# First tokens' softmax on ScalarE, weight shift on ScalarE, another load order, and last sums that end tile by tile

## The chip, the core and the metric

The kernel runs on one core of a Trainium2 chip. TensorE (PE) multiplies matrices, VectorE (DVE) and ScalarE (ACT) work on tiles, GpSimd (POOL) does a little of that too, and SyncE (SP) issues the transfers (DMA). The metric is the device time of one execution in microseconds; less is better. Three timed runs of the kernel before gave a median of 584.38 us (581.32 to 584.8).

## The reference

Attention over 4 batches, 8 heads, 576 tokens of width 64: a causal softmax, mixed by a gate with a memory read; its output, as 2304 tokens of width 512, goes through two weight layers with a squared ReLU between them. Both weights are float64.

```python
scores = where(causal, -1e9, q @ k.T / 8)
scores = scores - scores.max(-1)
a = exp(scores); a /= a.sum(-1) + 1e-9
phi = lambda x: where(x > 0, x, exp(x) - 1) + 1
mem_out = (phi(q) @ M_prev) / ((phi(q) * z_prev).sum(-1) + 1e-6)
x = g * mem_out + (1 - g) * (a @ v)        # g = sigmoid(beta), per head
r = maximum(x @ w_in, 0); out = (r * r) @ w_out
```

## The kernel before

**Staging.** All loads and stores are issued from SP, in one queue. The first 64 tokens of each batch (the only ones with a 64 x 64 score block) are handled apart in `first_tokens`, in two groups of two batches (g = 0, 1); they are the first block of 256 tokens for the two weight layers, so that TensorE has a block to work on while attention goes on. The other 512 tokens of each batch go through `attention`, in eight blocks of 256 for the layers (`moe`); the last two blocks are done together, 512 tokens wide, in `moe_pair`.

**Weights.** TensorE multiplies in a rounded float32 form, so each weight is split into a high and a low part, and a product is three matmuls (high x high, high x low, low x high). A piece n is 128 x 512 float64, loaded raw, as pairs of 32-bit words. `split_weight` makes a float32 of it: VectorE shifts the low word right by 29 (L163), ScalarE rescales the high word (L164), VectorE joins the two (L165), ScalarE rounds to the high part (L168), VectorE subtracts for the low part (L169). There are 32 pieces: pieces 0 to 3 are w_in and 4 to 7 w_out for the first quarter of the hidden width, and so on. Twelve fit into the first stage (9 `raw` tiles, two `hw`, one `xw` in two halves).

**First tokens.** For each group: `scores` (L265), `phi` (exp at L272, minimum at L273, then products and the gate's scale up to L280), `softmax` (scale and mask L285, maximum L288, subtraction L289, exp L290, sum L291, reciprocal and scale L292 to L295), `outputs` (transposes L304, copies L306, products L315, high part `xh` L319, low part `xl` L320). The two groups fill the two halves of `xh` and `xl`. The first layer matmuls of the first block (`up`, L721 to L723) need both halves: L721 and L723 read `xh`, L722 reads `xl`.

**What sets the order.** A planner places every instruction of all engines at build time, in one fixed order per engine; `first_tokens` has high priority in it, and `merge` interleaves attention, weight pieces and the first block. The loads of the first tokens come in the order that `SEQ` spells: a (q, k), b (q rows and z), c (v and M) of a group, g the gates, r a raw weight piece, l the first attention batch.

**The end.** `moe_pair` adds up four token tiles of 128 x 512 over 16 steps f. Tiles 0 and 1 have PSUM tiles of their own (`oacc`); tiles 2 and 3 are halves of one tile (`oacs`), and a reader of it waits for both. ScalarE copies the sums out (L692) and SP stores them (L694). GpSimd makes the low part `gl` there (L679).

## Time and profile before

| | |
|---|---|
| median of three runs | 584.38 us |
| the profiled execution | 583.52 us, its span 581.7 us |
| granted TensorE clock, mean | 0.997 of full speed |
| PE busy | 544.9 us (94%) |
| DVE, ACT busy | 406.3 us (70%), 349.3 us (60%) |

The span runs from the first to the last instruction; the rest of an execution's time lies around it. A matmul's duration reaches past the start of the next one, so that PE reads as busy when matmuls follow one another without a hole. A duration on the other engines overlaps a little with the next instruction too: what one costs a full queue is the distance from its start to the start of the one behind it. A share over the whole span says little here, since the first 46 us, the middle and the last 5 us have different limits.

### The profile page before, as it was taken

What the parts mean: (1) busy time and instruction counts of PE and PEld (TensorE: products, weight loads), DVE (VectorE), ACT (ScalarE), POOL (GpSimd) and SP (SyncE); (2) the same over time, 40 slices, a digit from 0 to 9 for tenths busy, and PEclk for the clock granted to TensorE, in tenths of its full rate; (3) what the DMA queues carried; (4) which work ended last, traced back from release to release, by engine and by line L of the source; (5) the groups of instructions that cost most, each with busy time, mean ns of one, the idle gap of its engine ahead of it and who ended that gap; (6) DMA issues with size and microseconds to landing.
All of it is one profiled execution on the core that took longest, in us unless ns stands there. A gap on an engine that the chain in (4) does not pass through costs nothing.

```text
span 581.7 us, 11097 instructions
## 1 busy us (share of the span) xinstructions
PE 544.9 (94%) x4019; PEld 469.7 (81%) x4019; DVE 406.3 (70%) x1338; ACT 349.3 (60%) x794; POOL 39.4 (7%) x36
## 2 busy tenths in 40 slices
...
GB/s 283 372 176 368 94 254 194 155 143 158 96 153 135 117 134 189 148 200 155 128 136 95 148 99 155 111 178 139 55 90 114 110 16 1 36 1 0 1 0 73
DMA packets 125462, 75.72 MB, mean 130 GB/s; under 512 B 97248, under 2 KB 110560, under 8 KB 125408
## 3 DMA queue, kind: packets, MB, share of 16 engines
...
q14 instruction: 23, 0.19, 0.1%
...
## 4 chain that ended last, share of the span: by engine, by line
PE 62%; DVE 22%; DMA 9%; ACT 4%; issue 2%; SPq 1%; ACTq 0%; DVEq 0%
PE oacc L713 6%; PE oacc L711 6%; PE oacc L712 6%; PE up L723 6%; PE up L722 6%; PE up L721 6%; PE sp L467 4%; DVE e L486 3%; PE up L672 2%; PE up L671 2%; PE up L670 2%; DVE a L546 2%; DMA aT<-a 2%; DVE w L169 2%; PE pm L435 2%
## 5 line engine op out<-in xcount | busy, mean ns | idle before, releaser
L721 PE MATMUL up<-xh,w 128*128 128x256 f32 x448 | 129.0, 288 | 0.9 <-ACT xh L319 0.7
L723 PE MATMUL up<-xh,w 128*128 128x256 f32 x448 | 129.3, 289 | 0.0
L722 PE MATMUL up<-xl,w 128*128 128x256 f32 x448 | 128.3, 286 | 0.3 <-DVE xl L320 0.3
L506 ACT ACTIVATE e<-e,mx 128x320 f32<-128x320 f32 (+3 forms) x128 | 77.7, 610 | 54.9 <-DVE memx L586 35.4
L721 PEld LDWEIGHTS up<-xh,w 128*128 128x128 f32 x448 | 86.3, 193 | 5.0 <-ACT xh L319 1.0
L711 PE MATMUL oacc<-w,gh 128*128 128x512 f32 x224 | 90.2, 403 | 0.0
L712 PE MATMUL oacc<-w,gh 128*128 128x512 f32 x224 | 88.9, 397 | 0.0
L722 PEld LDWEIGHTS up<-xl,w 128*128 128x128 f32 x448 | 86.2, 192 | 3.0 <-issue 0.6
L723 PEld LDWEIGHTS up<-xh,w 128*128 128x128 f32 x448 | 86.2, 192 | 1.3 <-issue 0.7
L713 PE MATMUL oacc<-w,gl 128*128 128x512 f32 x224 | 85.4, 398 | 0.8 <-DVE gl L733 0.8
L546 DVE SCALAR_TENSOR_TENSOR a<-e,a 128x128 f16<-128x128 f32 x116 | 66.0, 577 | 24.1 <-ACT a L544 23.6
L678 DVE CAST gh<-r 128x512 fp32r<-128x512 f32 x16 | 6.8, 428 | 78.6 <-ACT r L677 78.6
L544 ACT ACTIVATE a<-e 128x128 f16<-128x128 f32 x116 | 55.1, 525 | 9.5 <-DMA aT<-a 9.1
L727 ACT ACTIVATE r<-up 128x512 f32<-128x512 f32 x56 | 32.9, 588 | 42.6 <-PE up L723 25.2
L713 PEld LDWEIGHTS oacc<-w,gl 128*128 128x128 f32 x224 | 40.9, 188 | 9.3 <-DVE gl L733 1.9
L711 PEld LDWEIGHTS oacc<-w,gh 128*128 128x128 f32 x224 | 42.2, 188 | 7.5 <-ACT hw L164 0.8
L712 PEld LDWEIGHTS oacc<-w,gh 128*128 128x128 f32 x224 | 42.3, 189 | 6.6
L486 DVE CUSTOM_DVE_ANT_0 e<-sp,mask 128x320 f32<-128x320 f32 (+3 forms) x128 | 47.2, 415 | 0.0
L676 ACT ACTIVATE r<-up 128x512 f32<-128x512 f32 x16 | 9.6, 599 | 62.1 <-PE up L672 62.1
L679 POOL TENSOR_TENSOR gl<-r,gh 128x512 fp32r<-128x512 f32 x16 | 20.7, 1292 | 379.9 <-DVE gh L678 379.9
L733 DVE TENSOR_TENSOR gl<-r,gh 128x512 fp32r<-128x512 f32 x56 | 39.1, 699 | 2.9 <-ACT gh L730 1.7
L576 PE MATMUL acc<-vs,aT 128*128 128x128 f16 x302 | 36.5, 220 | 0.0
(153 smaller groups left out, 1131.1 us busy)
## 6 DMA issues: line engine op xcount, KB each, us to landing
...
```

Source lines behind the costliest of these rows:

```text
L486: nc.vector.tensor_tensor_reduce(out=e[:, h, ka:kb], in0=sps[:, h, cs], in1=mask[:, 448 - q0 + ka : 448 - q0 + kb], scale=-0.125, scalar=3 ...
L506: ex = nc.scalar.activation(e[:n, h, :ke], e[:n, h, :ke], AF.Exp, bias=bs, scale=-1.0, accum_out=sm[:n, h : h + 1])
L544: nc.scalar.mul(av[:, :, o0 : o0 + w], x, SC)
L546: nc.vector.scalar_tensor_tensor(out=av[:, :, o0 + w : o0 + 2 * w], in0=x, scalar=SC, in1=av[:, :, o0 : o0 + w], op0=ALU.mult, op1=ALU.sub ...
L576: nc.tensor.matmul(o2, aT[:, h * nb + c, :n], vs[:, h, c], start=False, stop=c == i)
L711: nc.tensor.matmul(acc[t], gh[:, u, ts], w_out_op(f, 0), start=f == 0, stop=False)
L712: nc.tensor.matmul(acc[t], gh[:, u, ts], w_out_op(f, 1), start=False, stop=False)
L713: nc.tensor.matmul(acc[t], gl[:, u, ts], w_out_op(f, 0), start=False, stop=f == NF - 1)
L721: nc.tensor.matmul(up[:, u, :], w_in_op(f, k, 0), xh[:, k, :], start=k == 0, stop=False)
L722: nc.tensor.matmul(up[:, u, :], w_in_op(f, k, 0), xl[:, k, :], start=False, stop=False)
L723: nc.tensor.matmul(up[:, u, :], w_in_op(f, k, 1), xh[:, k, :], start=False, stop=k == NK - 1)
L733: (nc.vector if n in GLV else nc.gpsimd).tensor_tensor(out=gl, in0=r, in1=gh.bitcast(F32), op=ALU.subtract)
```

## The change

Five edits, and what the planner makes of them.

- `split_weight`: for pieces 0 to 7 the shift of the low word is done by ScalarE (an Identity activation that reads the word's upper 16 bits and scales them down), for the others by VectorE as before. `half` is its constant bias.
- `phi`: the exp and VectorE's minimum become two ScalarE passes (ReLU of -q, then exp of its negative).
- `softmax`: scores are negated, VectorE takes a minimum instead of a maximum; the subtraction, exp and sum are sixteen ScalarE passes of 64 columns (8 for each group), each with the row's minimum as its bias and a sum as second output. VectorE's subtraction and sum are gone.
- `SEQ`: raw weight pieces are loaded between the tensors of the first tokens.
- `moe_pair`: each of the four token tiles has a PSUM tile of its own; in the last three steps the sums end one tile after another, and each tile is copied out and stored as it ends; `gl` is made by VectorE.

```diff
--- before.py
+++ after.py
@@ -11,6 +11,7 @@
 F16 = mybir.dt.float16
 BF16 = mybir.dt.bfloat16
 U32 = mybir.dt.uint32
+U16 = mybir.dt.uint16
 AF = mybir.ActivationFunctionType
 ALU = mybir.AluOpType
 AX = mybir.AxisListType
@@ -53,7 +54,7 @@
 KB = 1
 XB = 2
 PJ = 6
-SEQ = 'a0 b0 g a1 b1 c0 c1 r l r r r r'
+SEQ = 'a0 b0 g a1 r b1 r c0 l r r c1'
 W0 = 9
 EARLY = 'dp'
 LATE = 'dd'
@@ -104,6 +105,8 @@
     nc.scalar.copy(identr, idt)
     identb = cp.tile([P, P], BF16, name="identb")
     nc.vector.tensor_copy(identb, idt)
+    half = cp.tile([P, 1], F32, name="half")
+    nc.vector.memset(half, 2.0**-14 - 0.5)
     mask = cp.tile([P, MW], BF16, name="mask")
     nc.gpsimd.memset(mask, 0.0)
     nc.gpsimd.affine_select(
@@ -160,7 +163,11 @@
             u0, u1 = rw[:, :, 0], rw[:, :, 1]
             f1 = u1.bitcast(F32)
             hi, lo = wp[n][:, 0, c0:c1], wp[n][:, 1, c0:c1]
-            nc.vector.tensor_scalar(out=u0, in0=u0, scalar1=29, scalar2=None, op0=ALU.logical_shift_right)
+            if n < 8:
+                top = rw.bitcast(U16).rearrange("p n (t h) -> p n t h", h=2)[:, :, 0, 1]
+                nc.scalar.activation(u0, top, AF.Identity, scale=2.0**-13, bias=half[:, :1])
+            else:
+                nc.vector.tensor_scalar(out=u0, in0=u0, scalar1=29, scalar2=None, op0=ALU.logical_shift_right)
             nc.scalar.activation(f1, f1, AF.Prelu, scale=2.0**-111, alpha=-(2.0**32))
             nc.vector.scalar_tensor_tensor(
                 out=u1, in0=u1, scalar=3, in1=u0, op0=ALU.logical_shift_left, op1=ALU.bitwise_or
@@ -269,8 +276,8 @@
             wt0[g] = tp.tile([P, GN, P], F32, tag="w", name="w", bufs=2)
             f = wt0[g][:, :, D:]
             t2 = tp.tile([P, GN], F32, tag="t2", name="t2", bufs=2)
-            nc.scalar.activation(f, qn, AF.Exp)
-            me[g].tensor_scalar(out=f, in0=f, scalar1=1.0, scalar2=None, op0=ALU.min)
+            nc.scalar.activation(f, qn, AF.Relu, scale=-1.0)
+            nc.scalar.activation(f, f, AF.Exp, scale=-1.0)
             nc.vector.scalar_tensor_tensor(out=f, in0=qn, scalar=0.0, in1=f, op0=ALU.max, op1=ALU.add)
             ze[g].tensor_tensor(out=zb, in0=zb, in1=f, op=ALU.mult)
             nc.vector.reduce_sum(out=t2, in_=zb, axis=AX.X)
@@ -283,13 +290,15 @@
             e = wt0[g][:, :, :D]
             t1 = tp.tile([P, GN], F32, tag="t1", name="t1", bufs=2)
             nc.vector.scalar_tensor_tensor(
-                out=e, in0=sp[g], scalar=0.125, in1=mask0[:, None, :].to_broadcast(bc), op0=ALU.mult, op1=ALU.add
+                out=e, in0=sp[g], scalar=-0.125, in1=mask0[:, None, :].to_broadcast(bc), op0=ALU.mult, op1=ALU.subtract
             )
-            nc.vector.reduce_max(out=t1, in_=e, axis=AX.X)
-            xe[g].tensor_tensor(out=e, in0=e, in1=t1[:, :, None].to_broadcast(bc), op=ALU.subtract)
-            nc.scalar.activation(e, e, AF.Exp)
-            nc.vector.reduce_sum(out=t1, in_=e, axis=AX.X)
-            nc.vector.tensor_scalar(out=t1, in0=t1, scalar1=1e-9, scalar2=None, op0=ALU.add)
+            nc.vector.tensor_reduce(out=t1, in_=e, axis=AX.X, op=ALU.min)
+            ts = tp.tile([P, GN], F32, tag="ts", name="ts", bufs=2)
+            for i in range(GN):
+                nc.scalar.activation(
+                    e[:, i], e[:, i], AF.Exp, bias=t1[:, i : i + 1], scale=-1.0, accum_out=ts[:, i : i + 1]
+                )
+            nc.vector.tensor_scalar(out=t1, in0=ts, scalar1=1e-9, scalar2=None, op0=ALU.add)
             nc.vector.reciprocal(t1, t1)
             nc.vector.tensor_tensor(out=t1, in0=t1, in1=g1b, op=ALU.mult)
             ye[g].tensor_tensor(out=e, in0=e, in1=t1[:, :, None].to_broadcast(bc), op=ALU.mult)
@@ -652,17 +661,24 @@
     def moe_pair():
         xs = xq.pop()
         xh, xl = ([x[k // 2][:, k % 2].rearrange("p n c -> p (n c)") for k in range(NK)] for x in xs)
-        acc = [ps.tile([P, DM], F32, tag="acc", name="oacc", bufs=2) for _ in range(2)]
-        more = ps.tile([P, 2, DM], F32, tag="s", name="oacs")
-        acc += [more[:, 0], more[:, 1]]
+        acc = [ps.tile([P, DM], F32, tag=t, name="oacc", bufs=2) for t in ("acc", "acc", "av", "av")]
         pend = []
 
-        def down(f, gh, gl):
-            for t in range(4):
+        def down(f, gh, gl, tokens=range(4)):
+            mms = []
+            for t in tokens:
                 ts = slice(t * P, (t + 1) * P)
-                nc.tensor.matmul(acc[t], gh[:, ts], w_out_op(f, 0), start=f == 0, stop=False)
-                nc.tensor.matmul(acc[t], gh[:, ts], w_out_op(f, 1), start=False, stop=False)
-                nc.tensor.matmul(acc[t], gl[:, ts], w_out_op(f, 0), start=False, stop=f == NF - 1)
+                for g, part, s0, s1 in ((gh, 0, f == 0, False), (gh, 1, False, False), (gl, 0, False, f == NF - 1)):
+                    mms.append(nc.tensor.matmul(acc[t], g[:, ts], w_out_op(f, part), start=s0, stop=s1))
+            return mms
+
+        def evict(t):
+            b, blk = blocks[NBLK - 2 + t // 2]
+            r0 = b * S + QT[1 + 2 * blk + t % 2][0]
+            pool, tag, bufs = (mo, "x", XB) if t < 2 else (at, ("qh", "ql")[t - 2], 1)
+            o = pool.tile([P, DM], F32, tag=tag, name="o", bufs=bufs)
+            nc.scalar.activation(o, acc[t], AF.Copy, scale=WSC)
+            nc.sync.dma_start(out[r0 : r0 + P, :], o)
 
         for f in range(NF):
             up = ps.tile([P, 2 * BLK], F32, tag="up", name="up", bufs=2)
@@ -671,27 +687,32 @@
                 nc.tensor.matmul(up, w_in_op(f, k, 0), xl[k], start=False, stop=False)
                 nc.tensor.matmul(up, w_in_op(f, k, 1), xh[k], start=False, stop=k == NK - 1)
             r = mo.tile([P, 2 * BLK], F32, tag="r", name="r", bufs=RB)
-            gh = mo.tile([P, 2 * BLK], F32R, tag="gh", name="gh", bufs=GHB)
-            gl = mo.tile([P, 2 * BLK], F32R, tag="gl", name="gl", bufs=GLB)
+            if f < NF - 1:
+                gh = mo.tile([P, 2 * BLK], F32R, tag="gh", name="gh", bufs=GHB)
+                gl = mo.tile([P, 2 * BLK], F32R, tag="gl", name="gl", bufs=GLB)
+            else:
+                gh, gl = (at.tile([P, 2 * BLK], F32R, tag=t, name="gz") for t in ("kh", "kl"))
             nc.scalar.activation(r, up, AF.Relu, scale=WSC)
             nc.scalar.activation(r, r, AF.Square)
             nc.vector.tensor_copy(gh, r)
-            nc.gpsimd.tensor_tensor(out=gl, in0=r, in1=gh.bitcast(F32), op=ALU.subtract)
+            nc.vector.tensor_tensor(out=gl, in0=r, in1=gh.bitcast(F32), op=ALU.subtract)
             pend.append((f, gh, gl))
             yield
-            if len(pend) > 1:
+            if f == NF - 2:
+                down(*pend[0], tokens=(2, 3))
+            elif 0 < f < NF - 2:
                 down(*pend.pop(0))
-                yield
-        for x in pend:
-            down(*x)
-        for m in range(2):
-            b, blk = blocks[NBLK - 2 + m]
-            for t in range(2):
-                pool, tag, n = (mo, "x", XB) if m == 0 else (at, ("qh", "ql")[t], 1)
-                o = pool.tile([P, DM], F32, tag=tag, name="o", bufs=n)
-                nc.scalar.activation(o, acc[2 * m + t], AF.Copy, scale=WSC)
-                r0 = b * S + QT[1 + 2 * blk + t][0]
-                nc.sync.dma_start(out[r0 : r0 + P, :], o)
+            yield
+        three, two, one = pend
+        ends = None
+        for x, tokens in ((three, (0, 1)), (two, (0, 1)), (one, (0, 1)), (two, (2,)), (one, (2,)), (two, (3,)), (one, (3,))):
+            mms = down(*x, tokens=tokens)
+            if ends is not None:
+                tc.add_manual_dep(mms[0].ins, ends.ins.name, AFTER, reason="one token tile ends behind another")
+            ends = mms[-1]
+            if x is one:
+                for t in tokens:
+                    evict(t)
         yield
 
     def moe(n):
```

ScalarE, from the first group's exp (before) or the second group's (after) on; `raw` and the numbered `w` tiles are weight pieces, `w` without a number holds the first tokens' phi and softmax, `ts` their sums, `pe` and `e` belong to attention. Before:

```order
L272 ACTIVATE w<-tr_119 128x8x64
L164 ACTIVATE raw_141<-raw_141 128x512
L380 ACTIVATE pe<-qm 128x256
L290 ACTIVATE w<-w 128x8x64 x2
L164 ACTIVATE raw_149<-raw_149 128x512
L168 CAST w_98<-raw_141 128x512
L164 ACTIVATE raw_151<-raw_151 128x512
L164 ACTIVATE raw_153<-raw_153 128x512
L506 ACTIVATE e,sm<-e,mx 128x320
L164 ACTIVATE raw_155<-raw_155 128x512
L506 ACTIVATE e,sm<-e,mx 128x320
L168 CAST w_99<-raw_149 128x512
```

Now:

```order
L279 ACTIVATE w<-tr_121 128x8x64
L280 ACTIVATE w<-w 128x8x64
L175 CAST w_100<-raw_138 128x512
L168 ACTIVATE raw_143<-raw_143,half 128x512
L171 ACTIVATE raw_143<-raw_143 128x512
L298 ACTIVATE w,ts<-w,t_212 128x64 x8
L298 ACTIVATE w,ts<-w,t_260 128x64
L389 ACTIVATE pe<-qm 128x256
L298 ACTIVATE w,ts<-w,t_260 128x64 x4
L175 CAST w_101<-raw_143 128x512
L298 ACTIVATE w,ts<-w,t_260 128x64
L168 ACTIVATE raw_152<-raw_152,half 128x512
L171 ACTIVATE raw_152<-raw_152 128x512
L298 ACTIVATE w,ts<-w,t_260 128x64 x2
```

Between the first two pieces' casts there stood two exps; now there stand two of the new shifts and most of the sixteen pieces, interleaved with the weights.

VectorE, the last rows ahead of the second half of `xl`, which the first full group of `up` matmuls needs. Before:

```order
L444 TENSOR_TENSOR memx<-pm,nm 128x256
L165 SCALAR_TENSOR_TENSOR hw<-hw 128x512
L390 SCALAR_TENSOR_TENSOR pe<-qm,pe 128x256
L486 ISA e,mx<-sp,mask 128x192
L486 ISA mx 128x1
L163 TENSOR_SCALAR hw<-hw 128x512
L486 ISA e,mx<-sp,mask 128x192
L486 ISA mx 128x1
L320 TENSOR_TENSOR xl<-xp,xh 128x4x128
```

Now:

```order
L176 TENSOR_TENSOR w_108<-raw_437,w_108 128x512
L451 RECIPROCAL nm<-nm 128x4
L176 TENSOR_TENSOR w_111<-xw,w_111 128x256 x2
L495 ISA e,mx<-sp,mask 128x192
L495 ISA mx 128x1
L495 ISA e,mx<-sp,mask 128x192
L495 ISA mx 128x1
L176 TENSOR_TENSOR w_109<-hw,w_109 128x512
L399 SCALAR_TENSOR_TENSOR pe<-qm,pe 128x256
L453 TENSOR_TENSOR memx<-pm,nm 128x256
L329 TENSOR_TENSOR xl<-xp,xh 128x4x128
```

Ahead of `xl` stood attention's rows and two rows of one `hw` piece; now the low parts (`L176`) of three weight pieces stand there, and each of them waits for ScalarE's cast of that piece.

TensorE, the last down projections; `gh` and `gl` are the high and low part of a step's squared ReLU, `gz` those of the last step. Before, the last step's rows:

```order
L663 MATMUL oacc<-w_1140,gh 128x512
L664 MATMUL oacc<-w_1140,gh 128x512
L663 MATMUL oacc<-w_1140,gh 128x512
L664 MATMUL oacc<-w_1140,gh 128x512
L663 MATMUL oacs<-w_1140,gh 128x512
L664 MATMUL oacs<-w_1140,gh 128x512
L665 MATMUL oacc<-w_1140,gl 128x512 x2
L665 MATMUL oacs<-w_1140,gl 128x512
L663 MATMUL oacs<-w_1140,gh 128x512
L664 MATMUL oacs<-w_1140,gh 128x512
L665 MATMUL oacs<-w_1140,gl 128x512
```

Now, the last two steps' rows:

```order
L672 MATMUL oacc<-w_1153,gh 128x512 x4
L672 MATMUL oacc<-w_1153,gl 128x512 x2
L672 MATMUL oacc<-w_1154,gz 128x512 x6
L672 MATMUL oacc<-w_1153,gh 128x512 x2
L672 MATMUL oacc<-w_1153,gl 128x512
L672 MATMUL oacc<-w_1154,gz 128x512 x3
L672 MATMUL oacc<-w_1153,gh 128x512 x2
L672 MATMUL oacc<-w_1153,gl 128x512
L672 MATMUL oacc<-w_1154,gz 128x512 x3
```

The four tiles used to end 5, 4, 3 and 0 matmuls ahead of the last one, and the copy of the third waited for the fourth; now they end 13, 12, 6 and 0 ahead.

## Rows read from the trace of the kernel before

**Rows 1.** The page, part 1: busy time of each engine.

```profile
PE 544.9 (94%) x4019; PEld 469.7 (81%) x4019; DVE 406.3 (70%) x1338; ACT 349.3 (60%) x794; POOL 39.4 (7%) x36
```

**Rows 2.** Windows: length, busy of PE, PEld, DVE, ACT, POOL, clock, DMA share, GB/s.

```profile
10.00:15.00 5.00, 1.72 (x32) 1.53 (x30) 3.86 (x10) 0.63 (x1) 0.00 (x0) 1.00 1.03 383
15.00:20.00 5.00, 2.08 (x8) 1.27 (x8) 5.00 (x12) 3.30 (x6) 1.73 (x1) 1.00 1.03 408
45.00:50.00 5.00, 4.66 (x26) 4.45 (x26) 5.00 (x17) 5.00 (x15) 0.00 (x0) 0.66 1.03 417
50.00:60.00 10.00, 10.00 (x75) 8.70 (x74) 9.32 (x27) 9.25 (x23) 1.22 (x1) 1.00 0.72 268
100.00:150.00 50.00, 46.86 (x372) 39.31 (x373) 44.12 (x139) 36.03 (x78) 4.03 (x3) 1.00 0.62 146
500.00:560.00 60.00, 60.00 (x266) 49.68 (x265) 4.70 (x11) 13.54 (x22) 14.22 (x11) 1.00 0.00 1
```

**Rows 3.** Timeline of VectorE: start us, duration us, line, operation, tiles.

```profile
12.30 0.68 DVE L285 SCALAR_TENSOR_TENSOR w<-sp,mask 128x512 f32<-128x512 f32 x1
...
29.08 0.42 DVE L163 TENSOR_SCALAR raw<-raw 128x512 uint32<-128x512 uint32 x1
...
29.42 0.68 DVE L165 SCALAR_TENSOR_TENSOR raw<-raw 128x512 uint32<-128x512 uint32 x1
...
30.02 0.15 DVE L555 RECIPROCAL sm<-sm 128x2 f32<-128x2 f32 x1
...
41.97 0.43 DVE L163 TENSOR_SCALAR hw<-hw 128x512 uint32<-128x512 uint32 x1 [0.97 <-DMA hw<-in_w_in_dram]
...
45.36 0.68 DVE L320 TENSOR_TENSOR xl<-xp,xh 128x512 fp32r<-128x512 f32 x1
```

**Rows 4.** Windows, of ScalarE alone to the second `xh`, of VectorE to the second `xl`.

```profile
10.48:43.41 32.93, 22.17 (x48) 1.00 0.77 287
...
12.30:46.04 33.74, 32.67 (x91) 1.00 0.78 292
```

**Rows 5.** Timeline of ScalarE.

```profile
22.44 0.56 ACT L506 ACTIVATE e<-e,mx 128x320 f32<-128x320 f32 x1 [1.18 <-DVE mx L486]
...
22.91 0.19 ACT L506 ACTIVATION_READ_ACCUMULATOR e<-e,mx 128x1 f32 x1
...
23.00 0.66 ACT L164 ACTIVATE raw<-raw 128x512 f32<-128x512 f32 x1
...
25.08 0.45 ACT L506 ACTIVATE e<-e,mx 128x192 f32<-128x192 f32 x1
...
25.52 0.67 ACT L164 ACTIVATE raw<-raw 128x512 f32<-128x512 f32 x1
...
27.94 0.68 ACT L164 ACTIVATE raw<-raw 128x512 f32<-128x512 f32 x1
...
28.51 0.66 ACT L168 CAST w<-raw 128x512 fp32r<-128x512 f32 x1
```

**Rows 6.** Timeline of TensorE.

```profile
9.75 1.97 PE L265 MATMUL sp<-tr 64*64 64x64 f32 x32 [3.33 <-DMA tr<-in_t_dram]
...
32.78 2.08 PE L467 MATMUL sp<-kd,qm 64*128 64x320 f32 x8
...
46.09 0.41 PE L722 MATMUL up<-xl,w 128*128 128x256 f32 x1 [0.34 <-DVE xl L320]
...
53.10 1.13 PE L467 MATMUL sp<-kd,qm 64*128 64x320 f32 x8
```

**Rows 7.** Timeline of the end: last matmul, last copies, last stores issued.

```profile
576.78 0.39 PE L665 MATMUL oacs<-w,gl 128*128 128x512 f32 x1
...
577.20 1.08 ACT L692 ACTIVATE o<-oacs 128x512 f32<-128x512 f32 x2
...
576.69 1.96 SPq L694 DMA_DIRECT2D out_dram<-o  x4
```

**Rows 8.** The line that stores the last rows: issue to landing.

```profile
DMA to landing us min/median/max: 2.0/2.2/2.3
```

## The prediction

> **What bounds the kernel now.** I read the page first: TensorE is busy in 544.9 of 581.7 us [rows 1], so either its work or its holes decide. The windows tell where the holes are [rows 2]. From 50 us on TensorE is full; the only stretch with a visible loss is 100 to 150 us, 46.86 of 50. Before that it is nearly empty: 2.08 us of work between 15 and 20, while VectorE is busy in every one of those microseconds. TensorE's matmuls are the same before and after, so the end moves with the moment from which TensorE is full, with the holes behind it, and with what follows the last matmul.
>
> That moment is the second half of `xl`. VectorE starts it at 45.36, it takes 0.68, and the first `up` matmul that reads it starts at 46.09 [rows 3, 6]. From 12.30 to 46.04 VectorE is busy in 32.67 of 33.74 us [rows 4]; nearly all of the rest is one wait of 0.97 us for an `hw` load [rows 3]. ScalarE, which shares the weight pieces with it, is busy for 22.17 of the 32.93 us up to the second `xh` at 43.41 [rows 4]. So VectorE bounds the start, ScalarE has some 10 us to spare, and the change moves work from the one to the other.
>
> **Prices.** On VectorE a shift costs the queue 0.34 us (29.08 to 29.42) and a full 512-column pass 0.60 (29.42 to 30.02) [rows 3]. On ScalarE a 512-column pass costs 0.57 (27.94 to 28.51) [rows 5]. A piece of 64 columns with a bias and a sum is not in the trace. Its relatives are attention's exps: 320 columns take the queue 0.56 (22.44 to 23.00), 192 take 0.44 (25.08 to 25.52) [rows 5], hence 0.12 per 128 columns, and 0.44 - 0.12 = 0.32 for 64. Its far end upwards is 0.64, the 0.45 of the 192-column row and the 0.19 of a read of the sum that nothing hides (of the one at 22.91, 0.10 lies beside the next row) [rows 5]; downwards 0.20, if half of the 0.26 that the line leaves at no columns lies beside the next piece. I take 0.32, two rows of the same form on a line.
>
> **VectorE, alone.** Eight shifts go: 8 x 0.34 = 2.7. The two minima go (one input, taken at 0.34 as the shift): 0.7. Two subtractions and two sums: 4 x 0.60 = 2.4. That is 5.8 us; with `hw` loaded in time another 1.0. Were VectorE the only bound, `xl` would be ready at 46.0 - 6.8 = 39.2.
>
> **ScalarE.** It gets 8 shifts x 0.57 = 4.6, 16 pieces x 0.32 = 5.1 and one more pass over q within this stretch (the first group's runs ahead of it) = 0.6, and loses two full exps, 1.1. Its 22.2 us become 31.4. It can't start on these before the first raw piece is there. That load now stands right behind the second group's q and k, which land at 9.75 [rows 6]; 0.52 MB at the 383 GB/s of that window [rows 2] is 1.4 us, so 11.1. The second `xh` is then written at 11.1 + 31.4 = 42.5 at the earliest, `xl` at 43.2. ScalarE has become the bound of the start, and 2.8 us is the most that this part can give, at these prices.
>
> The Trainium skill speaks against the move: "ScalarE: Activation LUTs", section "Rules for kernel authors", gives minimum, addition and multiplication to VectorE, and budgets about 0.3 us for an activation and 0.83 ns for each element. By that budget a piece is 0.35 us, sixteen are 0.5 us more than I sum, an estimate from that page. The rows bear the rule out on price, 0.34 against 0.57 for a shift.
>
> **The two together.** They hand each piece to and fro (shift, rescale, join, round, subtract), so I walked both queues in their new order. Behind ScalarE's cast of the fifth piece stand some 7.5 us of its own rows up to the second `xh`, so that cast ends at 42.5 - 7.5 = 35.0. VectorE's low part of that piece waits for it, and from there to `xl` VectorE has 26 rows: ten full passes, 6.0, one shift, 0.3, and attention's and half-width rows, some 3.7 as they stand today; 10.0 in all, no wait among them. That is 45.0; counting ScalarE's rows by their distances and not by their busy time makes it 44.4. I take 44.7, a gain of 1.3 to 1.4 on 46.04. Ahead of the `up` matmul TensorE now also does the scores of a third attention batch, which it did at 53.10 in 1.13 us [rows 6]: 1.1 us that it need not do later, less up to 1.0 if it does them at the slow clock (2.08 at 32.78, same eight matmuls). The start gives 1.4 + 0.6 = **2.0 us**, between -3.1 (pieces at 0.64: 16 x 0.32 = 5.1 lost) and 6.8 (VectorE alone).
>
> **Loads.** The first group's c and the second group's b come later by one or two raw pieces, 1.4 to 2.8 us. The products that need c stand behind the softmax and the transposes, which are later than that in either order, and the pass over the second group's q would stand behind ScalarE's two rows for the first raw piece anyway: no price. If that cover went, VectorE would idle for up to 1.4 us at about 12. A later attention batch's kd no longer holds the `hw` loads back in SP's queue; that is the 0.97 us counted above.
>
> **The end.** The last matmul starts at 576.78 and ScalarE's two last copies run from 577.20 to 578.28 [rows 7], the third held up by the fourth. With a tile of its own the third is copied six matmuls earlier, and one copy, 0.54, is left behind the last matmul. The last store then has the transfer engines to itself: 2.0 instead of up to 2.3 us to landing [rows 8]. Together 0.54 + 0.2 = **0.7 us**, bounds 0.5 (no faster landing) and 0.9 (0.3 faster). `gl` on VectorE costs nothing: VectorE is busy for 4.70 of 60 us there [rows 2]. In the last step two tiles' sums of each of the two steps before it, 12 matmuls, cover the squared ReLU.
>
> **Sum.** 2.0 + 0.7 = 2.7 us off the profiled execution's 583.5 (its span 581.7 and 1.8 around it): **580.8 us**. That execution lies 0.9 below the median of the runs, whose own scatter is 3.5 us; a measurement of this kernel can't tell less than about 1%, 5.8 us, from no change.
>
> **Rivals.**
>
> *VectorE was the whole bound.* If a piece costs 0.20, ScalarE sheds 1.9 us and VectorE's 6.8 come out nearly whole; holes behind 100 us, 3.1 us in [rows 2] and mostly waits for VectorE, may shrink with it. For it: VectorE's 32.67 of 33.74. Against: ScalarE's sum. 583.5 - 6.8 - 0.7 = 576.0, or 578.4 with two thirds of the start's part.
>
> *Given back later.* The planner has laid out all engines anew: in the new order many of attention's scores stand behind more of the blocks' matmuls than before, while VectorE and ScalarE stay nearly full (9.32 and 9.25 of 10 at 50 to 60 us) [rows 2]. If the holes at 100 to 150 us grow from 3.1 to 5.1, only the end's gain is left: 582.8. For it: nothing fills VectorE's queue less there; against: both queues reach that stretch as early as TensorE does.
>
> *ScalarE makes the start later.* The pieces cost 0.64, ScalarE writes `xh` 5.1 us later than summed, and TensorE fills at 583.5 + 3.1 - 0.7 = 585.9 in terms of the end: slower. It decides above 0.32 + 2.7 / 16 = 0.49 per piece. Against it: the overlap of 0.10 in attention's row. The skill's rule above points this way, but its own budget stays below 0.49.
>
> *The clock.* Between 45 and 50 us the granted clock is 0.66 on the mean: TensorE, after a nearly idle stretch, gets 1.2 of 2.4 GHz and then the full one [rows 2]. With its work spread otherwise over 20 to 44 us, the slow stretch may last twice as long: 5 x (1 - 0.66) = 1.7 us lost once more, 582.5. The Trainium skill, "TensorE: Matmul & The Clock Gate", section "The HAM clock gate", has the throttled state as the default that activity lifts, and this trace's 0.66 agrees.
>
> That the change doesn't do what it says is excluded for the edits by the new order, which shows all 24 shifts and pieces on ScalarE ahead of the second `xh`.
>
> **Chances.** Forecast (start and end as summed, 579 to 582.4) 0.47; VectorE the whole bound 0.20; given back 0.18; ScalarE later 0.08; the clock 0.07. Of the second, nearly all lies beyond 1%, with a little of the first: faster 0.21. Slower by over 1% needs 590, twice the ScalarE rival's loss: 0.03. Within 1%: 0.76. The range leaves out the lower half of the second case and most of the fourth: 577.0 to 584.8.
>
> **What would show it.** Right: the first `up` matmul on `xl` at about 44.7, VectorE with 1 to 3 us of waits for ScalarE between 12 and 44, ScalarE busy for over 30 us up to the second `xh`; one copy behind the last matmul. Wrong: `xl` before 42 (pieces cheaper, or ScalarE's queue not in the way), after 46 (pieces dearer), or 44.7 with more than 3.1 us of holes at 100 to 150.

## The result: 589.14 us, slower by 0.9%

On one chip the changed kernel took 589.14 us (median of 5 runs, 586.76 to 590.87) and the kernel before 584.38 (581.32 to 584.95 in five runs there): a ratio of 1.0089 [1.006, 1.0118]. The forecast was 580.8 with a range of 577.0 to 584.8; the time lies above it. The profiled executions are 589.14 and 583.52 us, their spans 587.3 and 581.7. Later runs were made on other chips, each beside the kernel before, so only ratios are compared across them. The mean granted clock of the five runs is 0.981 to 0.987; that of the kernel before, in the runs beside the experiments, is 0.992 to 1.000.

### The profile page after: what moved, and what is told of

Same layout as the page of the kernel before. It is cut to its first block, busy times and chain, and to the rows that moved or that the text cites. A ratio compares the mean times of both kernels' runs of the same rounds, so it can differ in the third digit from the quotient of the medians.

```text
span 587.3 us, 11133 instructions
## 1 busy us (share of the span) xinstructions
PE 550.1 (94%) x4019; PEld 474.6 (81%) x4019; DVE 412.3 (70%) x1341; ACT 358.6 (61%) x834; POOL 15.5 (3%) x20
## 4 chain that ended last, share of the span: by engine, by line
PE 67%; DVE 12%; DMA 10%; ACT 9%; issue 2%; SPq 1%; ACTq 0%; DVEq 0%
PE oacc L672 7%; PE up L742 7%; PE up L743 7%; PE up L744 7%; PE oacc L732 6%; PE oacc L734 6%; PE oacc L733 6%; PE sp L476 5%; DMA aT<-a 3%; PE up L688 2%; PE up L687 2%; PE up L686 2%; PE acc L585 2%; DMA qm<-in_qv_dram 2%; PE pm L444 2%
## 5 line engine op out<-in xcount | busy, mean ns | idle before, releaser
L732 PE MATMUL oacc<-w,gh 128*128 128x512 f32 x224 | 89.8, 401 | 1.8 <-ACT gh L751 1.8
L733 PE MATMUL oacc<-w,gh 128*128 128x512 f32 x224 | 88.4, 395 | 0.0
L555 DVE SCALAR_TENSOR_TENSOR a<-e,a 128x128 f16<-128x128 f32 x116 | 64.7, 576 | 30.4 <-ACT a L553 29.9
L672 PE MATMUL oacc<-w,gh 128*128 128x512 f32 x120 | 36.8, 389 | 0.0
```

What stands on the lines that cost most here:

```text
L555: nc.vector.scalar_tensor_tensor(out=av[:, :, o0 + w : o0 + 2 * w], in0=x, scalar=SC, in1=av[:, :, o0 : o0 + w], op0=ALU.mult, op1=ALU.sub ...
L672: mms.append(nc.tensor.matmul(acc[t], g[:, ts], w_out_op(f, part), start=s0, stop=s1))
L732: nc.tensor.matmul(acc[t], gh[:, u, ts], w_out_op(f, 0), start=f == 0, stop=False)
L733: nc.tensor.matmul(acc[t], gh[:, u, ts], w_out_op(f, 1), start=False, stop=False)
```

## The profile after

The page, part 1, busy time of each engine, to be read against [rows 1]:

```profile
PE 550.1 (94%) x4019; PEld 474.6 (81%) x4019; DVE 412.3 (70%) x1341; ACT 358.6 (61%) x834; POOL 15.5 (3%) x20
```

The same 4019 matmuls keep TensorE busy for 5.2 us longer, so part of the loss is slower matmuls and not waiting. The windows, with the columns of [rows 2] (busy of PE, PEld, DVE, ACT, POOL, then the clock), say where:

```profile
25.00:30.00 5.00, 3.99 (x38) 3.05 (x36) 2.93 (x9) 5.00 (x13) 0.00 (x0) 1.00 1.04 396
30.00:35.00 5.00, 4.64 (x38) 3.01 (x39) 3.92 (x9) 5.00 (x10) 0.00 (x0) 1.00 0.23 75
35.00:40.00 5.00, 0.52 (x18) 0.38 (x14) 5.00 (x11) 5.00 (x13) 0.00 (x0) 0.99 0.86 289
40.00:45.00 5.00, 3.46 (x13) 2.35 (x14) 5.00 (x18) 5.00 (x17) 1.29 (x1) 0.50 1.01 385
45.00:50.00 5.00, 5.00 (x23) 4.65 (x22) 5.00 (x14) 3.86 (x7) 0.00 (x0) 0.50 1.02 413
50.00:60.00 10.00, 8.34 (x49) 7.29 (x49) 9.80 (x28) 8.82 (x23) 0.84 (x1) 0.82 0.39 124
100.00:150.00 50.00, 48.41 (x385) 41.14 (x384) 38.74 (x125) 33.23 (x71) 4.23 (x3) 1.00 0.60 127
200.00:300.00 100.00, 97.11 (x795) 84.81 (x793) 84.26 (x289) 68.74 (x153) 0.00 (x0) 1.00 0.68 145
```

Some of these stretches before:

```profile
20.00:25.00 5.00, 0.00 (x0) 0.00 (x0) 5.00 (x19) 3.82 (x11) 0.00 (x0) 1.00 1.04 412
25.00:30.00 5.00, 0.00 (x0) 0.00 (x0) 5.00 (x16) 4.71 (x11) 0.00 (x0) 1.00 0.58 221
35.00:40.00 5.00, 3.57 (x47) 2.93 (x46) 5.00 (x11) 4.27 (x11) 0.00 (x0) 1.00 0.82 247
```

TensorE now works early (25 to 35 us), is nearly empty at 35 to 40, and then runs at half clock: 1.2 of 2.4 GHz from 39.94 to 53.6 us by the trace's clock record, 13.65 us, against 46.32 to 49.74 (3.41 us) before. The work of 100 to 150 us, which the prediction watched for holes, is fuller than before (48.41 against 46.86).

The clock record leaves out the start of a run. It has 1.00 there, and yet in the kernel before the eight transposes of the first group take nearly twice as long as the eight of the second, which are of the same size:

```profile
30.91 1.94 PE L304 MATMUL px<-identr,w 128*128 128x128 f32 x8 [12.73 <-ACT w L168]
...
36.44 1.09 PE L304 MATMUL px<-identr,w 128*128 128x128 f32 x8
```

Their starts lie 0.21 us apart and then 0.11: TensorE runs at half rate up to some 35 us in the kernel before, and up to 33 us in the changed one (its eight transposes at 19.48 take 1.94 us as well). What is called slow clock here is the time behind this, from the record.

ScalarE's timeline (start, duration, line, operation), a shift, two pieces, the weight rows ahead of the second `xh`, and that `xh`:

```profile
11.04 0.76 ACT L168 ACTIVATE raw<-raw,half 128x512 uint32<-128x512 uint16 x1 [2.86 <-DMA raw<-in_w_in_dram]
11.69 0.66 ACT L171 ACTIVATE raw<-raw 128x512 f32<-128x512 f32 x1
12.25 0.62 ACT L279 ACTIVATE w<-tr 128x512 f32<-128x512 f32 x1
...
15.20 0.34 ACT L298 ACTIVATE w<-w,t 128x64 f32<-128x64 f32 x1
15.44 0.19 ACT L298 ACTIVATION_READ_ACCUMULATOR w<-w,t 128x1 f32 x1
15.54 0.33 ACT L298 ACTIVATE w<-w,t 128x64 f32<-128x64 f32 x1
...
36.58 0.65 ACT L175 CAST w<-raw 128x512 fp32r<-128x512 f32 x1
37.14 0.68 ACT L171 ACTIVATE hw<-hw 128x512 f32<-128x512 f32 x1
...
38.85 0.64 ACT L175 CAST w<-raw 128x512 fp32r<-128x512 f32 x1
39.39 0.67 ACT L535 COPY aF<-pxa 64x128 f32<-64x128 f32 x3
...
41.78 0.57 ACT L328 CAST xh<-xp 128x512 fp32r<-128x512 f32 x1
```

VectorE's `xl` (against 45.36 in [rows 3]), and TensorE from the second group's products (L324) on, with what ended the idle time before a row in brackets (against [rows 6]):

```profile
44.32 0.68 DVE L329 TENSOR_TENSOR xl<-xp,xh 128x512 fp32r<-128x512 f32 x1
```

```profile
34.72 0.80 PE L324 MATMUL xp<-wx,tr 128*64 128x64 f32 x20
40.12 1.06 PE L530 MATMUL pxa<-identr,e 128*64 128x128 f32 x4 [4.59 <-ACT aF L535]
...
43.18 2.08 PE L476 MATMUL sp<-kd,qm 64*128 64x320 f32 x8 [0.20 <-DVE mx L495]
45.05 3.23 PE L574 MATMUL acc<-vv,aF 64*128 64x64 f32 x12
...
48.04 0.56 PE L743 MATMUL up<-xl,w 128*128 128x256 f32 x1
...
57.74 1.45 PE L574 MATMUL acc<-vv,aF 64*128 64x64 f32 x8 [1.66 <-ACT aF L535]
```

The products that `xh` needs end at 35.5, and `xh` is written from 41.78 on: for 6 us it stands behind weight rows in ScalarE's queue. So does the copy `aF` for the second attention batch, and TensorE waits 4.59 us for that. What then follows runs at half clock: eight scores in 2.08 us (1.13 at full clock in [rows 6]), twelve products in 3.23. `xl` is there at 45.0, and the first `up` on it starts at 48.04.

The end, against [rows 7]:

```profile
582.24 0.60 ACT L680 ACTIVATE o<-oacc 128x512 f32<-128x512 f32 x1 [0.50 <-PE oacc L672]
...
582.72 0.84 PE L672 MATMUL oacc<-w,gz 128*128 128x512 f32 x3
583.60 0.60 ACT L680 ACTIVATE o<-oacc 128x512 f32<-128x512 f32 x1 [0.76 <-PE oacc L672]
```

One copy is left behind the last matmul, which starts at 583.18: 4.1 us to the end of the span, 4.9 before.

**Lag.** To see where the time goes I add up, at an instant of the kernel before, the matmuls still to come, each at its usual duration at full clock, and look for the instant at which another kernel has as much left. The difference is its lag (a minus is a lead). Of the changed kernel it is -1.4 us at 46, +3.4 at 60, +6.0 at 400 and +6.4 at the last matmul; the end gives 0.8 back, and 5.6 is the difference of the spans. At 46 us the lag depends on what the short matmuls are priced at, where a kernel has done others of them by then: with each form at its mean distance to the next start it is +0.3 for the changed kernel, -3.9 for e3 below (-6.2 in the table) and -4.5 for e8 (-6.0). At 60 us that moves nothing by more than 0.3, at 400 us by up to 0.8.

## The experiments

All ran beside the kernel before. "Slow" is the time at 1.2 GHz before 70 us, from the trace's clock record, in us; lags, in us, are those of the profiled execution.

```
run                       ratio [95%]               slow    lag at  46     60    400    last
(before)                                            3.41
(changed)                 1.0089 [1.0060, 1.0118]  13.65         -1.4   +3.4   +6.0   +6.4
e1  end alone             0.9993 [0.9969, 1.0016]   6.83         -0.5   +0.5   +0.3   +0.3
e2  24 matmuls added      1.0074 [1.0047, 1.0102]   6.83         -0.6   +0.5   +4.4   +3.7
e3  no shift              1.0005 [0.9979, 1.0031]  10.24         -6.2   +0.9   +3.8   +3.9
e4  old softmax           1.0121 [1.0093, 1.0150]  10.24         +2.3   +4.1   +6.8   +6.7
e5  changed, again        (one run, 588.14)        17.07         -1.4   +5.0   +5.5   +5.4
e6  softmax + end         1.0078 [1.0048, 1.0108]  17.07         -0.5   +6.2   +7.5   +7.0
e7  old loads             1.0151 [1.0123, 1.0180]  20.48         +2.0   +5.8   +8.2   +8.8
e8  no shift, 12 added    1.0022 [0.9999, 1.0045]   6.83         -6.0   -0.7   +0.7   +0.6
e9  new loads + end       0.9938 [0.9913, 0.9962]   3.41         -0.5   -0.9   -1.7   -1.9
e10 third batch late      1.0069 [1.0048, 1.0091]  10.24         +0.7   +1.8   +4.7   +3.9
e11 e3, third batch late  1.0044 [1.0020, 1.0068]   6.83         -2.7   -1.7   +4.7   +4.1
e12 e9, 12 added          1.0132 [1.0106, 1.0158]  10.24         +6.5   +6.8   +7.4   +6.9
e13 xh first              1.0136 [1.0083, 1.0188]  17.07         -1.8   -0.3   +9.6   +9.2
e14 third load order      1.0135 [1.0092, 1.0177]   6.83         +1.7   +1.3   +9.8   +9.2
e15 fourth load order     0.9966 [0.9946, 0.9986]   0            -1.4   -3.2   -1.5   -1.5
e16 half the softmax      0.9961 [0.9927, 0.9994]   3.41         -0.3   +1.6   -0.6   -0.4
e17 pieces + end          1.0035 [1.0010, 1.0059]  17.07         -1.5   +3.7   +4.5   +4.6
e18 four shifts           1.0186 [1.0150, 1.0222]   6.83         +2.1   +2.4  +12.3  +13.1
```

Three profiled executions are 2 to 3 us longer than the median of their runs: e3 (586.6 against 583.65), e6 (589.72 against 587.35) and e18 (596.53 against 593.49). That is why e3 has a lag of +3.9 beside a ratio of 1.0005. Behind 70 us the record has further slow stretches that the column leaves out: 10.24 us in e13 (106 to 123), and 3.41 us each in e2 (at 130), e3 (107), e8 (368), e11 (229), e17 (112) and e18 (153). The changed kernel, in both profiles, and e14 have none there, so their loss behind 70 us is not the clock's.

**e1: the end alone.** The kernel before with the new `moe_pair`; everything ahead of the pair stands in the old order.

```diff
 def moe_pair():
-    more = ps.tile([P, 2, DM], F32, tag="s", name="oacs")
+    acc = [ps.tile([P, DM], F32, tag=t, name="oacc", bufs=2) for t in ("acc", "acc", "av", "av")]
...
```

> The kernel before with the change to the last sums alone (own PSUM tile for each token tile, last three steps tile by tile, gl on VectorE). All orders are those of the kernel before up to the last pair of blocks. In the changed kernel the time from the last matmul's start to the end of the span fell from 4.92 to 4.12 us. Theory: this part gives that and nothing else, 0.8 us off the span (580.9), and the whole loss of the change lies in the first 400 us. Rival: gl on VectorE or the new PSUM tiles hold the last matmuls up, then the last matmul starts later than at 576.8 and the time is the same or above.

582.11 us beside 582.03: no difference that can be measured. In the trace the last matmul starts 4.1 us before the span's end, not 4.9, so the 0.8 is there and is smaller than what a comparison sees. The slow clock of this run is 6.83 us in the very order that had 3.41: it varies by some us from one execution to another.

**e2: the empty stretch filled.** Matmuls whose sum nobody reads, ahead of the second group's products.

```diff
 def outputs(g):
+    if g == 1:
+        dm = ps.tile([P, DM], F32, tag="acc", name="warm", bufs=2)
+        for _ in range(24):
+            nc.tensor.matmul(dm, identr, xl[:, :, :P], start=True, stop=True)
...
```

> The changed kernel with 24 matmuls of 128x512 added whose sums nobody reads; 19 of them stand in TensorE's queue right behind the first tokens' last products (at 35.5 us in the changed kernel) and ahead of the transposes that waited until 40.1 us. Clock theory: the 4.6 us hole there made the granted clock fall at 39.9 us, and the 13.65 us at 1.2 GHz, against 3.41 in the kernel before, cost (13.65 - 3.41) / 2 = 5.1 us; with the hole filled the clock stays up, and the last matmul starts 3 to 6 us earlier than in the changed kernel, a span of 581 to 584. Queue theory: the start is late because ScalarE's queue is too long, whatever the clock; then xl still ends at about 45.0 and the span stays within 1 us of 587.3, or grows by the 24 matmuls' 5.4 us.

The windows of e2, columns as above:

```profile
35.00:40.00 5.00, 5.00 (x41) 4.12 (x42) 5.00 (x12) 5.00 (x14) 0.00 (x0) 1.00 0.55 184
40.00:45.00 5.00, 4.32 (x24) 3.33 (x23) 5.00 (x17) 4.26 (x12) 1.24 (x1) 1.00 0.98 370
45.00:50.00 5.00, 5.00 (x37) 4.22 (x38) 5.00 (x18) 4.89 (x14) 0.00 (x0) 1.00 1.03 415
```

With TensorE busy at 35 to 40 the clock stays full where it was halved, and the lag from 65 to 120 us is under 1 instead of +3 to +4. That is the first part of the loss. But the lag is +2.8 at 130 and +4.4 at 400, the last matmul starts 2.7 us earlier than as changed, less than the 3 to 6 of the clock theory, and the time, 586.54 beside 582.03, is not told apart from the changed kernel's: a second part lies behind 60 us.

**e3, e4: one of the two moves undone.**

Both start from the changed kernel. e3 has all shifts on VectorE (the first two lines); e4 has `phi` and `softmax` as before.

```diff
-    if n < 8:
+    if n < 0:
...
-    nc.scalar.activation(f, qn, AF.Relu, scale=-1.0)
+    nc.scalar.activation(f, qn, AF.Exp)
...
```

> The changed kernel with the shift of all weight pieces back on VectorE; softmax on ScalarE, the load order and the last sums stay changed. ScalarE loses 8 x 0.65 = 5.2 us of queue ahead of the second xh, VectorE gets 8 x 0.34 = 2.7 us. Queue theory: ScalarE was the bound, so the second xh comes 3 to 5 us earlier than at 41.8 and the hole of TensorE ahead of it shrinks from 4.6 us to under 2; the clock theory then gives under 7 us at 1.2 GHz and a span of 580 to 584. Rival: the softmax pieces or the load order are to blame; then the hole and the slow stretch stay and the span is within 1 us of 587.

> The changed kernel with the first tokens' phi and softmax as before (minimum, subtraction and sum on VectorE, two full exps); shifts of eight pieces on ScalarE, the load order and the last sums stay changed. ScalarE loses 16 x 0.33 + 0.6 - 1.2 = 4.7 us ahead of the second xh, VectorE gets 3.1 us. Queue theory: the second xh comes 2 to 4 us earlier, and the span is 580 to 585. Rival, the shifts alone are to blame: no better than the changed kernel, 586 to 588.

583.65 and 589.61 us. At first sight the shifts cost 0.8% and the softmax nothing. e6, e9 and e14 show that this reading doesn't hold. What e3 does show: a lead at 46 us (-6.2 in the table) was gone at 56, where TensorE waits 1.80 us for VectorE's join of a raw piece and the clock is low once more (0.83 at 50 to 60 us).

**e5: the changed kernel again.**

> The changed kernel a second time, for a second profile. If its loss is a property of its order, both parts of it come again at the same places: ScalarE full from 15 to 35 us, TensorE nearly empty at 35 to 40 (0.52 of 5 in the first profile), 10 to 14 us at 1.2 GHz from about 40 on, and a lag behind the kernel before of 3 to 5 us at 100 us and of 4 to 6.5 us at the end. If the middle (120 to 375 us) is an accident of one execution, the lag changes there by 2 us or more in another place, and if the clock's stretch is one, it lasts under 7 us.

Its windows:

```profile
35.00:40.00 5.00, 2.02 (x26) 1.54 (x24) 5.00 (x11) 5.00 (x13) 0.00 (x0) 0.98 0.59 190
40.00:45.00 5.00, 3.46 (x13) 2.34 (x14) 5.00 (x18) 5.00 (x17) 1.30 (x1) 0.50 0.92 349
45.00:50.00 5.00, 5.00 (x23) 4.65 (x22) 5.00 (x15) 3.80 (x7) 0.00 (x0) 0.50 1.03 418
```

The start comes again: the first `up` on `xl` at 48.05, the slow clock from 39.83 for 13.65 us (and a further 3.41 at 60). From 60 to 400 us it adds 0.5 us, not 2.6: two executions of one order differ there by 2 us.

**e6, e7: the old load order.**

e6 is the kernel before with `phi`, `softmax` and `moe_pair` as changed, and no shift moved. e7 is the changed kernel with

```diff
-SEQ = 'a0 b0 g a1 r b1 r c0 l r r c1'
+SEQ = 'a0 b0 g a1 b1 c0 c1 r l r r r r'
```

> The kernel before with the softmax part and the end of the change; no shift on ScalarE and the old load order. Queue theory (the shifts fill ScalarE): ScalarE gets 16 pieces and a pass less two exps, some 4.6 us, and stays below full, so xl comes 1 to 4 us earlier than the 46.1 of before; what TensorE makes of that decides. If the second stage's loads and the clock take an early start back, as in the run with no shift, the end is at 582 to 584 (ratio 0.998 to 1.002); if that was the doing of the new load order, 578 to 581 (0.993 to 0.998). Rival, the newly laid out order costs 3 us or more between 120 and 375 us in any variant: 584 to 586.

> The changed kernel with the load order of before; all else as changed. If ScalarE's queue with the shifts in it sets the loss, it stays: 586 to 590, ratio 1.005 to 1.012, with TensorE nearly empty just ahead of 40 us and 10 us or more at 1.2 GHz. Rival, the load order (first raw pieces ahead of the second group's k) makes the stretch: 582 to 585, under 7 us at 1.2 GHz.

587.35 and 591.16 us beside 582.24. Both have TensorE short of work around 40 us (3.63 of 5 at 35 to 40 and 1.38 at 40 to 45 in e6, 3.22 and 3.08 in e7) and 17 and 20 us of slow clock. The softmax part, with the order that it brings, loses without any shift, so the loss doesn't need the shifts; and the new load order is better than the old one in both pairs (e3 against e6, changed against e7).

**e8: no shift, and 12 matmuls added** (the edit of e2 with `range(12)`, in e3).

> The run with no shift on ScalarE, with 12 matmuls of 128x512 added that nobody reads, ahead of the second group's products. Clock theory: they fill the empty stretch, the 1.2 GHz from 41.75 to 48.58 goes or moves to where TensorE waits anyway, and of the 7 us that this variant gave back between 46 and 56 us about 3 stay: 580 to 581.5, ratio 0.994 to 0.998. Rival, the loads of the second stage bound 50 to 58 us (ScalarE and VectorE waited there for raw pieces): an early start is worth nothing, 583 to 584.5, ratio 1.000 to 1.003, and the lag at 56 us is +0.5 to +1.5 again.

The clock, full until then, fell to 1.2 GHz at 50.6, after a stretch in which TensorE worked 2.92 of 5 us (45 to 50). The lead of 6.0 at 46 was 0.7 at 60. 583.65 beside 582.24: the time is the rival's, and the start's lead is given back by 60 us. The rival's reason isn't shown: between 45 and 58 us TensorE's longest wait is 2.1 us, for ScalarE's `r`, and no engine waits more than 0.2 us for a load; the slow clock came 9 us later than in e3 and its first stretch was as long (6.83 us).

**e9, e12: the new load order and the end alone**, and with 12 matmuls added.

Both start from e1.

```diff
-SEQ = 'a0 b0 g a1 b1 c0 c1 r l r r r r'
+SEQ = 'a0 b0 g a1 r b1 r c0 l r r c1'
```

> The kernel before with the new load order and the end of the change; softmax and shifts as before. In the pairs run so far the new load order is worth 3 to 4 us (softmax and end: 587.35 with the old order, 583.65 with the new; all of the change: 591.16 and 588.5). If it is worth that by itself (earlier raw pieces give ScalarE and VectorE their weight work ahead of the softmax), 578 to 580, ratio 0.990 to 0.996. Rival: it only mends what ScalarE's queue does wrong, and with ScalarE not full it is worth nothing: 581.5 to 583.5, ratio 0.998 to 1.003. Second rival, any newly laid out order costs 3 us: 584 to 586.

> The kernel with the new load order and the end alone, with 12 matmuls of 128x512 added that nobody reads ahead of the second group's products. Clock theory: the 3.4 to 6.8 us at 1.2 GHz from about 45 on are cut to 3.4 or none, 0.5 to 2 us less than the run without them: ratio 0.988 to 0.996. Rival: TensorE has no time for them or waits behind them (12 x 0.23 = 2.7 us, twice that at 1.2 GHz): the same or up to 2 us later than without.

e9 is 580.69 us beside 583.76, faster than both kernels by the ratios. Its windows:

```profile
35.00:40.00 5.00, 3.12 (x47) 2.56 (x44) 4.71 (x11) 3.48 (x8) 0.00 (x0) 1.00 0.80 270
40.00:45.00 5.00, 4.72 (x53) 3.72 (x52) 4.33 (x17) 4.53 (x15) 1.07 (x1) 1.00 1.00 390
45.00:50.00 5.00, 4.66 (x27) 4.39 (x25) 5.00 (x14) 4.45 (x14) 0.00 (x0) 0.66 1.03 412
```

Its `xl` ends at 45.51, later than the changed kernel's 45.0, yet it leads at 60 us by 0.9: TensorE's work stands close ahead of `up`, and the clock is halved for 3.41 us only. In e12 the added matmuls stood in the way: TensorE ran them from 39.09 to 43.5, ahead of the second group's products, the lag was +6.5 at 46, and the ratio of 1.0132 lies above both forecasts. Keeping an engine busy helps only where it has nothing else to do.

**e10, e11: the third attention batch late.** Its scores are laid out behind the first 24 `up` matmuls, in the changed kernel and in e3.

```diff
 def scores(group):
...
+    if third and order[2] == (b, p, tiles):
+        tc.add_manual_dep(mm.ins, third.pop().ins.name, AFTER, reason="the third batch comes late")
...
+    if (n, j) == (0, TJ):
+        third.append(mm)
...
```

> The changed kernel, with the third attention batch's scores laid out behind the first 24 up matmuls, as in the kernel before, and not ahead of them. If that batch coming early makes the hole of 1.66 us at 57.7 (TensorE's queue meets its products before ScalarE has copied aF), the hole goes and the lag at 60 to 100 us falls from 3.4 to 5 to some 1.5 to 3: 585 to 586.8, ratio 1.005 to 1.008. If ScalarE's full queue and the clock are all of it, the stretch at 1.2 GHz stays at 10 to 14 us from 40 on, holes only change places, and the time stays at 588 to 590 (1.009 to 1.013).

> The same edit to the run with no shift on ScalarE, which led by 6.2 us at 46 and had given all of it back at 56. If the third batch's early place is what gives it back, 3 us or more of the lead are left at 60 us: 579.5 to 581.5, ratio 0.994 to 0.998. If the loads of the second stage and the clock do (raw pieces land when they land, the clock falls when TensorE waits for them), the lag at 60 is 0 to +1.5 again: 583 to 585, ratio 1.000 to 1.005.

e10: 587.31 us, the lag at 60 falls from +3.4 to +1.8, which is in that theory's range. Its reason didn't come true: the hole at 57.7 is gone, but one of 1.60 us stands at 56.0 instead (for `gh`), as the other theory had it; what is shorter is the slow clock, 10.24 us against 13.65, worth 1.7 at half rate. e11: 586.45 beside 583.76, no better than e3; it led by 1.7 at 60 and lost 6.4 from there to 400. Both theories missed e11: the start was better, and the loss came later.

**e13: `xh` first.** ScalarE's casts of weight pieces 6 to 11 are laid out behind the second group's `xh`.

```diff
 def split_weight(n):
-    nc.scalar.copy(hi, f1)
+    cast = nc.scalar.copy(hi, f1)
+    if 12 > n >= 6:
+        tc.add_manual_dep(cast.ins, xhi[-1].ins.name, AFTER, reason="xh goes first")
...
```

> The changed kernel, with ScalarE's casts of weight pieces 6 to 11 laid out behind the second group's xh. Queue theory: xh no longer waits from 35.5 to 41.8 and is written at 36.5 to 38, xl at 38 to 40.5, the first up on xl starts at 39 to 41.5 (48.04 as changed), and the end comes 3 to 5 us earlier than as changed: 583.5 to 586, ratio 1.001 to 1.005. Rival (the middle, 60 to 400 us, ends as late in this order whenever the start comes): the lead at 46 us is there and is gone at 100 to 375, 586.5 to 589, ratio 1.007 to 1.011. Second rival, the casts now late are what up waits for: holes at 42 to 50.

`xh` came at 39.84 and not at 41.78, TensorE's products having become slower too (1.2 GHz from 31.33 for 17 us); the lead was 1.8 us at 46 and 0.3 at 60 to 100. Then 9.9 us were lost by 400, most of them between 100 and 125, with TensorE busy for 19.27 of 25 us at a clock of 0.80 (24.68 at full clock as changed). 591.94 us: later than either theory said.

**e14, e15: other load orders, nothing moved to ScalarE.**

e14 is the first of the new lines in e1, e15 the second.

```diff
-SEQ = 'a0 b0 g a1 b1 c0 c1 r l r r r r'
+SEQ = 'a0 b0 g a1 r b1 c0 c1 r l r r r'
+SEQ = 'a0 b0 g a1 b1 r c0 c1 r l r r r'
```

> The kernel before with the end of the change and a third load order: one raw piece ahead of the second group's b, the rest as before; nothing on ScalarE moved. If every newly laid out order loses 2 to 3 us between 60 and 400 us, 583.5 to 586.5, ratio 1.000 to 1.005. If only work moved to ScalarE does that, 579 to 582.5, ratio 0.992 to 0.998, as with the new load order.

> The same with a fourth load order: one raw piece between the second group's b and the two c; nothing on ScalarE moved. The theories give the same two ranges as for the third load order: 583.5 to 586.5 if laying out anew costs 2 to 3 us in itself, 579 to 582.5 if not.

591.95 and 582.09 us beside 583.91. One raw piece a place earlier or later decides between losing 1.4% and gaining 0.3%. The orders explain how so small an edit can matter: of TensorE's 4019 rows 4005 stand in e1's order in e15, 2570 in e14 (the longest sequence of rows that both traces have in the same order). In e14 VectorE and ScalarE do what they did before, and 8.5 us are lost from 60 to 400. Its stretch at 200 to 250 us, and TensorE's waits at 200 to 280 (us in total, times, longest):

```profile
200.00:225.00 25.00, 22.82 (x183) 19.66 (x182) 19.75 (x65) 15.51 (x34) 0.00 (x0) 1.00 0.76 138
225.00:250.00 25.00, 21.05 (x181) 17.58 (x180) 20.70 (x70) 17.79 (x39) 0.00 (x0) 1.00 0.68 161
```

```profile
PE vt L404 <- DVE s L578: 2.2, 1, 2.2
PE sp L467 <- DVE ql L365: 2.2, 1, 2.2
PE px L621 <- ACT r L739: 1.4, 1, 1.4
```

Three long waits, each for another instruction, at full clock. e15 had no slow clock behind the start (its eight transposes take 1.94 us at 30.21, 1.09 at 35.24):

```profile
45.00:50.00 5.00, 5.00 (x41) 4.67 (x39) 5.00 (x16) 5.00 (x15) 0.00 (x0) 1.00 1.03 413
```

It led by 3.2 us at 60 with 1.4 at 46: 1.7 of it is the half clock of 3.41 us that it didn't have.

**e16: half of the softmax**, the pieces of the first group only, in e9.

```diff
 def softmax(g):
+    if g == 0:
+        nc.vector.tensor_reduce(out=t1, in_=e, axis=AX.X, op=ALU.min)
...
+    else:
+        nc.vector.reduce_max(out=t1, in_=e, axis=AX.X)
...
```

> The new load order and the end, with the softmax part on ScalarE for the first group alone (8 pieces), where ScalarE had 2 us and more of gaps at 15 to 25 us; no shift there, the second group and the exps of q as before. If it is ScalarE's fullness ahead of the second xh that costs, this is free: VectorE sheds 1.2 us and the time is 579 to 581.5, ratio 0.990 to 0.996. If moving softmax work costs in any dose (half of the 0.67 per cent that the whole softmax part cost at this load order), 582 to 584, ratio 0.996 to 1.000.

581.71 us beside 583.91, ratio 0.9961: between the two ranges of time, and not told apart from e9.

**e17, e18: a part moved, the order meant to be kept.** e17 is e1 with the softmax's sixteen pieces on ScalarE; e18 is e15 with the shifts of four pieces there (`if n < 4`).

The first lines are e17's, the last two e18's.

```diff
...
-    nc.scalar.activation(e, e, AF.Exp)
-    nc.vector.reduce_sum(out=t1, in_=e, axis=AX.X)
+    for i in range(GN):
+        nc.scalar.activation(e[:, i], e[:, i], AF.Exp, bias=t1[:, i : i + 1], scale=-1.0, accum_out=ts[:, i : i + 1])
...
+    if n < 4:
+        nc.scalar.activation(u0, top, AF.Identity, scale=2.0**-13, bias=half[:, :1])
```

> The kernel before with the end of the change and the softmax's sixteen pieces on ScalarE (exps of q, shifts and load order as before), in an order close to that of before. If the pieces cost by themselves (ScalarE's queue, then the clock), the loss of the run with the whole softmax part and the old loads comes back: ratio 1.004 to 1.009, 584.3 to 587.3. If the loss is that of the order, the time is that of the kernel with the end alone or a little less, since VectorE sheds 2.4 us and more: ratio 0.994 to 1.001, 578.5 to 582.7.

> The run with one raw piece between the second group's b and the two c (ratio 0.9966), with the shifts of the first four weight pieces on ScalarE, in an order close to it. ScalarE gets 4 x 0.65 = 2.6 us, VectorE sheds 4 x 0.34 = 1.4. If shifts on ScalarE cost by themselves (half of what all eight seemed to cost, 1.8 per cent), ratio 1.003 to 1.008, 583.7 to 586.6; if the loss is that of the order, ratio 0.993 to 0.999, 578 to 581.5.

e17: 585.52 us beside 582.84, a ratio of 1.0035, just below the first theory's range of ratios and above the second's. Its start is the changed kernel's over again, without a single shift: the wait of TensorE, and the windows.

```profile
38.72 1.06 PE L523 MATMUL pxa<-identr,e 128*64 128x128 f32 x4 [3.36 <-ACT aF L528]
```

```profile
35.00:40.00 5.00, 1.64 (x19) 1.12 (x14) 5.00 (x11) 5.00 (x13) 0.05 (x1) 0.72 0.86 272
40.00:45.00 5.00, 2.72 (x12) 1.86 (x11) 5.00 (x20) 4.91 (x14) 1.31 (x1) 0.50 1.00 392
45.00:50.00 5.00, 5.00 (x24) 4.65 (x22) 5.00 (x13) 3.98 (x11) 0.00 (x0) 0.50 1.02 410
```

A lag of +3.7 at 60 and 0.8 more up to 400: here the cost comes at the start, and little behind it. e18 missed both ranges: 593.49 us, a ratio of 1.0186. It lost 2.4 us up to 60 and 9.9 from there to 400. In neither run was the order kept. In e18 3839 of TensorE's 4019 rows stand in e15's order, but only 584 of the 666 rows of ScalarE that both have and 1186 of VectorE's 1350; in e17, against e1, 3647 of 4019, 545 of 664 and 1113 of 1348, fewer still. So e17's cost is not the pieces' alone either.

## Why the prediction was wrong

**VectorE and ScalarE, alone and together: right.** A piece costs the queue 0.34 (0.32 summed). A shift costs 0.65 (11.04 to 11.69), not 0.57: 8 x 0.08 = 0.6 us more. ScalarE is busy for 31.28 us from 10.48 to the second `xh`'s end at 42.35 (31.4 and 42.5 summed), VectorE for 28.91 of the 32.70 from 12.30 to `xl` (3.8 us of waits, 1 to 3 expected), and `xl` ends at 45.0 (44.7). The walk through both queues held to 0.3 us, in part by luck: shifts and pieces cost 0.9 us more than summed (8 x 0.08 + 16 x 0.02), and ScalarE's other rows 1.0 less. Of the signs that were named, none of being wrong came (`xl` before 42 or after 46, more than 3.1 us of holes at 100 to 150); the one that failed is the first `up` on `xl`, at 48.04 and not 44.7. The estimate from the Trainium skill's "ScalarE: Activation LUTs" ("Rules for kernel authors"), 0.35 us a piece, agrees with the 0.34.

**"TensorE's matmuls are the same before and after, so the end moves with the moment from which TensorE is full ... That moment is the second half of `xl`": this step failed.** `xl` came 1.0 us earlier and the first `up` on it 1.95 later. The walk followed the two engines to `xl` and never followed TensorE's own queue between 20 and 46 us. There the freed VectorE lets the transposes and products run early (3.99 and 4.64 of 5 at 25 to 30 and 30 to 35 us; before, it had no work at all from 20 to 30), and `aF` and `xh`, which release the next ones, stand in ScalarE's queue behind weight rows. TensorE empties, its clock falls at 39.94, and the attention work ahead of `up` runs at half speed. What that cost is an estimate: of the 13.65 us it was busy for some 12, which at full clock would have been 6; before, 3.4 and 1.7. The difference is 4.3 us, and the hole at 57.74 adds 1.7. Without both the lag of +3.4 at 60 would be a lead of 2.6, against the 2.0 forecast. No run shows that lead: with the empty stretch filled (e2) the lag at 60 was +0.5, with 3.41 us of slow clock at 55.

**The third attention scores** were priced as a gain of 0.6; they ran at half clock in 2.08 us, the case for which up to 1.0 was set against them. In e10, laid out late, the lag at 60 fell by 1.6, with a slow stretch that was shorter by 3.41 us.

**The clock rival: the right mechanism at a third of its size.** It was "twice as long: 1.7 us lost once more", with a chance of 0.07, priced by the 5 us before. The slow stretch was four times as long in one profile and five in the other, and the granted clock was low in all five runs (0.981 to 0.987). That it follows the empty stretch is shown by e2, where filling it took the slow stretch at 40 to 54 away and the lag with it, and by e17, where the hole and the slow clock come together again. The Trainium skill ("TensorE: Matmul & The Clock Gate", section "The HAM clock gate") has the slow state as the default that activity lifts. The trace agrees that it lifts: here only at 53.6, after more than 8 us without a gap.

**Given back later: right that it happens, wrong in place.** 100 to 150 us, where it was looked for, became fuller. The changed kernel lost 2.6 us (0.5 the second time) between 60 and 400, in small waits at many places: TensorE's come to 7.3 us there, none over 1.3, against 4.0 before.

**Loads: "no price" was wrong as a price of zero.** The new load order, with the end and the order that it brought, gave -0.62% (e9), and it was better than the old one in both pairs. It isn't a price of the loads alone: another load order, with one raw piece moved, gave +1.35% (e14).

**The end: right.** 0.7 forecast, 0.8 in the trace of e1 and of the changed kernel, below what a comparison shows.

**Sum of the profiled execution:** +3.4 (start, to 60 us) + 2.6 (60 to 400) + 0.4 (400 to the last matmul) - 0.8 (end) = +5.6, the difference of the spans. Two smaller things in the prediction: two thirds of the start's part give 578.3, not 578.4, on which nothing hangs; and less than 1% could be told from no change, since 0.9% came with an interval of 1.006 to 1.0118.

**What stays open.** What decides the stretch from 60 to 400 us. From one order to another its part went from -2.2 (e16) to +9.9 (e13, e18), with or without work on ScalarE: +8.5 in e14, where nothing was moved. No run prices a moved part in a kept order; e17 and e18 were meant to and are not. So the differences e3, e4 and e6 make against the changed kernel are not prices of a shift or of the softmax: the order that came with each is in them. Shown, by e2, is what the empty stretch and the slow clock behind it did to the start; which part of it is due to the work moved and which to the new order is not. Whether e9, e15 and e16 differ isn't settled either; all three are faster than the kernel before.
